# Decode attention for 16 heads on one core: finer last V, first K in three pieces, and V14 rows dealt unevenly

## The chip, the cores and the metric

The kernel runs on one core of a Trainium2 chip. The metric is the device time of one execution in microseconds, the median of several runs; lower is better. Beside it stands one execution recorded by the hardware profiler, whose rows are the profile. The engines are TensorE (PE, its weight loads apart as PEld), VectorE (DVE), ScalarE (ACT), GpSimd (POOL) and SyncE (SP, which issues most transfers); 16 DMA engines move the data.

## The reference

One query row per head attends to 8192 keys. q is (1, 16, 1, 256), k and v are (1, 16, 8192, 256), all bf16.

```python
scale = q.shape[-1] ** -0.5
scores = jnp.einsum("bhqd,bhkd->bhqk", q, k) * scale
p = _softmax(scores, axis=-1)
return jnp.einsum("bhqk,bhkd->bhqd", p, v)
```

## The kernel before

A head's K is 4 MB and so is its V. Both are read from DRAM as 128 partitions of 64 keys ("columns" j = 0 to 63) of 256 values each, so one column is 128 x 512 bytes and a whole head is 32 KB in each partition. Two buffers hold K and two hold V (L86, L87), used by even and odd heads in turn.

**Scores.** VectorE takes columns 0 to 47: for each one a fused multiply with the broadcast q and a sum over the 256 values (L189), which gives one score per partition. TensorE takes columns 48 to 63 in four groups of four: it transposes them (L279), ScalarE copies the transposes from PSUM (L368), TensorE multiplies them with q (L293), and ScalarE copies the 16 scores to S (L372, semaphore "sc"). VectorE then takes the maximum over all 64 columns (L206), TensorE turns it into a row (L227), VectorE reduces it (L173), TensorE broadcasts it (L233), ScalarE forms the exponentials (L380).

**Output.** For each head TensorE runs 64 matmuls, one per column of V, into one PSUM accumulator (`pv`, L258); ScalarE scales the result by the reciprocal of the sum (L393) and sends 512 bytes out (L400).

**Order of the transfers.** One list, `stream` (L57 to L69), written by hand, is issued by SP in its order (L128 to L138). Most entries are a whole head. The first K is cut at column 16 (K_FIRST, L14), V0, V1 and V13 are halved, V14 is cut in four pieces of 16 columns and V15 in seven of 16, 16, 12, 8, 6, 4 and 2 columns (V_LATE, L16). Each late piece has a semaphore of its own (V_SEMS, L18). SP waits before an entry that reuses a buffer: for K, that VectorE is done with the head two before ("kd", L132) and that TensorE has transposed it ("tp", L133); for V, that the matmuls of the head two before are done ("pv", L135). All transfers have 128 rows, one per partition.

**Waits that the change touches.** `head` (L180 to L206) is VectorE's work on one K; it waits for the first piece, at column 16 of head 0 for the rest (L186 to L188), and ahead of the maximum for its own last product (L204) and for "sc" (L205). `pv` (L251) takes a table of waits by column, filled at L348 and L354; at column 32 of V13 and V1 there is one for the second half (L355). GpSimd counts the late semaphores up by 16 at the start (L166), so that the first turns of the loop do not stop at waits meant for the last one.

**q at the start.** ScalarE loads q (L402), TensorE transposes it (L316) and broadcasts each head's row over 128 partitions, two heads per PSUM bank (L328). ScalarE copies them to q_all (L405, L413) and, after the first pair, head 0's 258 columns to q_now (L363), where VectorE and TensorE read them.

Of the kernel before, what the change touches and what calls it, by code (L numbers as in the profile page):

```python
# [6 lines left out]
ACT = mybir.ActivationFunctionType  # L7
# [3 lines left out]

NPE = 16
GRP = 4
K_FIRST = 16  # L14
V_HALVED = 13
V_LATE = {14: (0, 16, 32, 48), 15: (0, 16, 32, 44, 52, 58, 62)}  # L16
AHEAD = {"kd": 1, "sc": 1, "sp": 2, "ex": 2, "m": 1, "g": 1, "mT": 1, "l": 2, "bc": 1, "nb": 1, "rc": 2, "pv": 2, "fin": 4}
V_SEMS = (("va0", "v0b", "v0c", "v0d"), ("va1", "v1b", "v1c", "v1d", "v1e", "v1f", "v1g"))  # L18


class _Step:
# [19 lines left out]
def bass_standalone__mha_softmax__decode_kernel(nc: bass.Bass, q: bass.AP, k: bass.AP, v: bass.AP, out: bass.AP):  # L41
    B, H, Sq, D = q.shape
    Sk = k.shape[2]
    P = 128
    J = Sk // P
# [3 lines left out]
    NG = NPE // GRP  # L49
    JD = J - NPE  # L50
    QW = D + NH
    HALF = J // 2
# [1 line left out]

    stream = [("k", 0, 0, K_FIRST, "k0"), ("k", 0, K_FIRST, J, "k0b"), ("k", 1, 0, J, "k1")]  # L57
    stream += [("v", 0, 0, HALF, "va0"), ("k", 2, 0, J, "k0"), ("v", 0, HALF, J, "v0c")]
    stream += [("v", 1, 0, HALF, "va1"), ("k", 3, 0, J, "k1"), ("v", 1, HALF, J, "v1c")]
    for h in range(2, H):  # L60
# [10 lines left out]
    with contextlib.ExitStack() as ctx:  # L71
# [9 lines left out]
        def sem(name):  # L81
            if name not in sems:
                sems[name] = ctx.enter_context(nc.semaphore(name))
            return sems[name]
# [3 lines left out]
        q_sb = sb("q_sb", [H, D], dt)  # L88
        q_all = sb("q_all", [P, (H + 1) * QW], dt)
        q_now = [sb(f"q_now{i}", [P, QW], dt) for i in range(2)]  # L90
# [3 lines left out]
        m = sb("m", [P, 2], FP32)  # L94
# [14 lines left out]
        sm = ps("sm", [P, 512])  # L109
        qps = ps("qps", [P, 512])  # L110

        for name in ("pool", "cb", "cf", "qp", "qs", "qb", "kd", "tp", "kt", "sp", "sc", "m", "mT", "g", "bc", "nb", "ex"):
            sem(name)
        for name in ("l", "rc", "pv", "fin", "ldq", "k0", "k0b", "k1", "va0", "va1", "v1h", "o0", "o1"):
            sem(name)
        late = [name for row in V_SEMS for name in row[1:] if name not in ("v0c", "v1c")] + ["v1h"]
        for row in V_SEMS:
# [3 lines left out]
        def src(t, h):  # L121
            return t[0, h].rearrange("(p j) d -> p (j d)", p=P)

        if True:

            @(lambda f: f(nc.sync))
            def _(sp):
                for kind, h, a, b, name in stream:  # L128
                    buf = (kbuf if kind == "k" else vbuf)[h % 2]
                    if h >= 2 and a == 0:  # L130
                        if kind == "k":
                            sp.wait_ge(sem("kd"), h)  # L132
                            sp.wait_ge(sem("tp"), (h - 1) * NG)  # L133
                        else:
                            sp.wait_ge(sem("pv"), h + 1)  # L135
                    sp.dma_start(  # L136
                        buf[:, a * D : b * D], src(k if kind == "k" else v, h)[:, a * D : b * D]
                    ).then_inc(sem(name), 16)  # L138
                sp.nop()

            @(lambda f: f(nc.gpsimd))
# [27 lines left out]
            @(lambda f: f(nc.vector))  # L169
            def _(dve):  # L170
                def xmax(h):
                    dve.wait_ge(sem("mT"), h.of(1, 2))
                    dve.tensor_reduce(g[0:1, h.par : h.par + 1], mx[0:1, 0:P], AX.X, ALU.max).then_inc(sem("g"), 1)  # L173

                def recips(h):
                    dve.wait_ge(sem("l"), h.of(1, 3))
                    dve.wait_ge(sem("fin"), h.of(1, 3))
                    dve.reciprocal(recip[0:1, h.par : h.par + 1], qps[0:1, 0:1]).then_inc(sem("rc"), 1)  # L178

                def head(h, at):  # L180
                    dve.wait_ge(sem("qb"), h.of(1, 1))
                    dve.wait_ge(sem("ex"), h.of(1, 1))
                    dve.wait_ge(sem(f"k{h.par}"), h.of(8, 16 - 8 * h.par))
                    buf = kbuf[h.par]
                    for j in range(JD):
                        if j == K_FIRST and h.par == 0:  # L186

                            dve.wait_ge(sem("k0b"), 16)  # L188
                        ins = dve.tensor_tensor_reduce(  # L189
                            out=buf[:, j * D : (j + 1) * D],  # L190
                            in0=buf[:, j * D : (j + 1) * D],
                            in1=q_now[h.par][:, 0:D],
                            scale=SCALE,
                            scalar=0.0,
                            op0=ALU.mult,
                            op1=ALU.add,
                            accum_out=S[h.par][:, j : j + 1],
                        )
                        if j in at:
                            at[j]()  # L200
                    ins.then_inc(sem("kd"), 1)
                    if JD in at:
                        at[JD]()
                    dve.wait_ge(sem("kd"), h.of(1, 2))  # L204
                    dve.wait_ge(sem("sc"), h.of(1, 2))  # L205
                    dve.tensor_reduce(m[:, h.par : h.par + 1], S[h.par][:, :], AX.X, ALU.max).then_inc(sem("m"), 1)  # L206

                with dve.Fori(0, H // 2) as i:  # L208
                    ev, od = _Step(0, i), _Step(1, i)
                    prev = od.back(2)  # L210

                    def later(f, h):
                        with dve.If(i > 0):
                            f(h)

                    head(ev, {2: lambda: later(recips, ev.back(2)), 40: lambda: later(xmax, prev)})
                    head(od, {2: lambda: later(recips, prev), 3: lambda: xmax(ev)})
                last = _Step(H - 1)
                recips(last.back(1))
                xmax(last)  # L220
                recips(last)

            @(lambda f: f(nc.tensor))
            def _(pe):
# [87 lines left out]

                pe.wait_ge(sem("ldq"), 16)
                pe.wait_ge(sem("cb"), 1)
                for hf in range(NH):
                    ins = pe.matmul(  # L316
                        qps[:, hf * H : (hf + 1) * H],
                        lhsT=q_sb[:, hf * P : (hf + 1) * P],
                        rhs=identb[0:H, 0:H],
                        start=True,  # L320
                        stop=True,
                    )
# [15 lines left out]
                with pe.Fori(0, H // 2 + 1) as i:  # L338
                    ev, od = _Step(0, i), _Step(1, i)
                    fin_turn = pe.snap((i // 8) * 16 + 16)  # L340
                    half_turn = pe.snap(((i + 1) // 8) * 16 + 16)
                    old = od.back(2)
                    with pe.If(i < H // 2):
                        scores(ev)
                    with pe.If(i > 0):
                        pv(
                            ev.back(2),
                            {V_LATE[14][n]: [(V_SEMS[0][n], fin_turn)] for n in range(1, len(V_SEMS[0]))},  # L348
                            {32: lambda: transpose_m(old), 48: lambda: bcast(old), 64: lambda: total(old)},
                        )  # L350
                    with pe.If(i < H // 2):
                        scores(od, before=ev)
                    with pe.If(i > 0):
                        waits = {V_LATE[15][n]: [(V_SEMS[1][n], fin_turn)] for n in range(1, len(V_SEMS[1]))}  # L354
                        waits[HALF].append(("v1h", half_turn))  # L355
                        pv(old, waits, {})
                    with pe.If(i < H // 2):
                        total(ev)

            @(lambda f: f(nc.scalar))  # L360
            def _(act):
                def q_copy(h, src_q):
                    act.activation(out=q_now[h.par][:, :], in_=src_q, func=ACT.Copy).then_inc(sem("qb"), 1)  # L363
# [25 lines left out]
                def final(h, dst):  # L389
# [10 lines left out]
                    act.dma_start(dst, o_sb[h.par][0:1, :]).then_inc(sem(f"o{h.par}"), 16)  # L400

                act.dma_start(q_sb[:, :], q[0, :, 0, :]).then_inc(sem("ldq"), 16)  # L402
                by_head = q_all[:, 0 : H * QW].rearrange("p (h w) -> p h w", w=QW)
                act.wait_ge(sem("qp"), 1)
                act.activation(  # L405
                    out=by_head[:, :, D:QW],
                    in_=qps[:, 0 : NH * H].rearrange("p (f h) -> p h f", f=NH),
                    func=ACT.Copy,
                    scale=SCALE,
                )  # L410
                for pair in range(H // 2):
                    act.wait_ge(sem("qp"), pair + 2)
                    ins = act.activation(  # L413
                        out=by_head[:, 2 * pair : 2 * pair + 2, 0:D],
                        in_=acc[pair % 2][:, :].rearrange("p (h d) -> p h d", h=2),
                        func=ACT.Copy,
                    ).then_inc(sem("qs"), 1)
                    if pair == 0:
                        act.wait_ge(sem("qs"), 1)
                        q_copy(_Step(0), q_all[:, 0:QW])  # L420
                act.wait_ge(sem("cf"), 4)
                flat = out.rearrange("b h s d -> (b s) (h d)")
                with act.Fori(0, H // 2) as i:
# [55 lines left out]
```

## Time and profile before

| what | value |
|---|---|
| three runs | 320.09, 320.12, 320.47 us (median 320.12) |
| the profiled execution's own time | 320.24 us |
| its span, first to last instruction | 318.8 us |
| mean granted TensorE clock | 0.85 |
| busy: PE / DVE / ACT / POOL | 215.7 / 275.1 / 92.5 / 1.6 us |
| read from DRAM | 134.23 MB, 421 GB/s over the span |

How to read the profile: times in it are microseconds from the start of the span. A row of a timeline or chain gives start, length, engine, source line, operation and the tiles written and read; behind it in brackets stands the idle time before it and what ended that. SPq rows are issues of transfers; a row "DMA issues" gives how many, KB each, and the time from issue to landing. Windows give the busy time of each engine in a stretch, then the granted PE clock, the mean busy share of the 16 DMA engines, and GB/s; a packet counts with all the time it is open, so a share can pass 1.

### The profile page before, as it was taken

Reading aid. Unit: us, or ns where it says so; the run is one execution under the profiler, and the core shown is the slowest. Engines: PE = TensorE matmul, PEld = TensorE weight load, DVE = VectorE, ACT = ScalarE, POOL = GpSimd, SP = SyncE. Lnnn points to the kernel's source line nnn. Section 1 sums busy time; section 2 is a strip of 40 time slices with the busy share of each in tenths; the row PEclk is TensorE's granted clock in tenths of the full one; section 3 lists DMA queues with packets and bytes.
Section 4 is the critical chain, followed back from the end, with each engine's and each line's share of the span. In section 5 each row is a group of like instructions: output and inputs, shape, how many; then the busy total and the mean of one; then the engine's idle time right before and its main releaser. Section 6 shows DMA issues by size and latency. Waiting matters only on the chain.

```text
span 318.8 us, 6855 instructions
## 1 busy us (share of the span) xinstructions
PE 215.7 (68%) x2162; PEld 154.4 (48%) x2162; DVE 275.1 (86%) x1584; ACT 92.5 (29%) x171; POOL 1.6 (0%) x11
## 2 busy tenths in 40 slices
PE   4427186885685947839388472975839567397996
PEld 1326164664353635626256352653627346265774
DVE  2899999999999998897979979889798897979920
ACT  5436050336015060420504214060230604106010
POOL 1000000000000000000000000000000000000000
PEclk9999999798598786968769598785968969588999
DMA  8999999999999999999999999999999999999994
GB/s 327 455 398 448 399 456 415 419 415 452 428 432 440 419 444 419 444 428 432 436 423 440 415 448 428 432 436 428 440 415 448 419 440 424 436 417 420 417 422 194
DMA packets 6549, 134.29 MB, mean 421 GB/s; under 512 B 752, under 2 KB 912, under 8 KB 1424
## 3 DMA queue, kind: packets, MB, share of 16 engines
q1 hardware_dynamic: 6480, 134.22, 98.5%
q8 instruction: 2, 0.03, 0.0%
q10 hardware_dynamic: 64, 0.02, 0.0%
q14 instruction: 3, 0.02, 0.0%
HBM read 134.23 MB, written 0.01 MB: 421 GB/s over the span
## 4 chain that ended last, share of the span: by engine, by line
DMA 52%; DVE 23%; PE 22%; issue 1%; ACT 1%; SPq 0%; DVEq 0%; ACTq 0%
DMA vbuf<-in_v_dram 48%; DVE kbuf L189 22%; PE acc L258 20%; DMA kbuf<-in_k_dram 4%; DVE S L189 1%; PE sm L233 1%; ACT KT L368 1%; PE mx L227 0%; PE tp L279 0%; SPq L136 0%; PE spe L293 0%; DVE g L173 0%; ACT o_sb L393 0%; DVE recip L178 0%; DVEq L208 0%
## 5 line engine op out<-in xcount | busy, mean ns | idle before, releaser
L189 DVE CUSTOM_DVE_ANT_0 kbuf<-kbuf,q_now 128x256 bf16<-128x256 bf16 x768 | 268.5, 409 | 22.4 <-DMA kbuf<-in_k_dram 21.4
L258 PE MATMUL acc<-vbuf,E 128*1 128x256 bf16 x1024 | 144.6, 310 | 45.2 <-DMA vbuf<-in_v_dram 45.1
L258 PEld LDWEIGHTS acc<-vbuf,E 128*1 128x1 bf16 x1024 | 94.8, 94 | 88.1 <-DMA vbuf<-in_v_dram 46.4
L368 ACT ACTIVATE KT<-tp 128x1024 bf16<-128x1024 bf16 x64 | 62.3, 1021 | 45.9 <-PE tp L279 45.4
L189 DVE DVE_READ_ACCUMULATOR2_ANT S<- 128x1 f32 x768 | 55.0, 72 | 0.0
L279 PE MATMUL tp<-identb,kbuf 128*128 128x128 bf16 x512 | 41.6, 236 | 13.6 <-DMA kbuf<-in_k_dram 13.4
L293 PE MATMUL spe<-q_now,KT 128*128 128x1 bf16 x512 | 22.9, 166 | 27.0 <-ACT KT L368 26.7
L279 PEld LDWEIGHTS tp<-identb,kbuf 128*128 128x128 bf16 x512 | 32.9, 106 | 17.0 <-DMA kbuf<-in_k_dram 11.2
L293 PEld LDWEIGHTS spe<-q_now,KT 128*128 128x128 bf16 x512 | 18.2, 99 | 35.4 <-ACT KT L368 26.4
L393 ACT ACTIVATE o_sb<-acc,recip 1x256 bf16<-1x256 f32 x16 | 7.3, 457 | 83.8 <-PE acc L258 82.6
L376 ACT ACTIVATE negb<-sm 128x1 f32<-128x1 f32 x16 | 2.8, 174 | 87.4 <-PE sm L233 87.4
L173 DVE TENSOR_REDUCE g<-mx 1x1 f32<-1x128 f32 x16 | 4.4, 276 | 7.0 <-PE mx L227 7.0
L227 PE MATMUL mx<-ident,m 128*1 128x128 f32 x32 | 6.3, 279 | 5.8 <-DVE m L206 5.8
L233 PE MATMUL sm<-g,ones_row 1*128 1x1 f32 x32 | 6.4, 268 | 4.7 <-DVE g L173 4.7
L233 PEld LDWEIGHTS sm<-g,ones_row 1*128 1x128 f32 x32 | 5.1, 198 | 6.8 <-DVE g L173 5.3
L363 ACT ACTIVATE q_now<-q_all 128x258 bf16 (+1 forms) x17 | 7.1, 418 | 0.2
L178 DVE RECIPROCAL recip<-qps 1x1 f32<-1x1 f32 x16 | 2.4, 152 | 3.9 <-PE qps L243 3.9
L380 ACT ACTIVATE E<-S,negb 128x64 bf16<-128x64 f32 x16 | 5.6, 348 | 0.5
L227 PEld LDWEIGHTS mx<-ident,m 128*1 128x1 f32 x32 | 2.2, 83 | 6.4 <-DVE m L206 6.0
L328 PE MATMUL acc<-q_sb,identb 16*128 16x256 bf16 x16 | 4.4, 403 | 1.0 <-ACT q_all L413 1.0
L413 ACT ACTIVATE q_all<-acc 128x512 bf16<-128x512 f32 x8 | 4.4, 593 | 0.9 <-PE acc L328 0.9
L372 ACT ACTIVATE S<-spe 128x16 f32<-128x16 f32 x16 | 2.9, 183 | 3.7 <-PE spe L293 3.7
(20 smaller groups left out, 17.1 us busy)
## 6 DMA issues: line engine op xcount, KB each, us to landing
kbuf<-in_k_dram SPq DMA_DIRECT2D x15, 4096.0 KB, 20.5
vbuf<-in_v_dram SPq DMA_DIRECT2D x11, 4096.0 KB, 29.1
vbuf<-in_v_dram SPq DMA_DIRECT2D x6, 2048.0 KB, 24.3
vbuf<-in_v_dram SPq DMA_DIRECT2D x6, 1024.0 KB, 12.9
kbuf<-in_k_dram SPq DMA_DIRECT2D x1, 3072.0 KB, 11.7
kbuf<-in_k_dram SPq DMA_DIRECT2D x1, 1024.0 KB, 4.8
vbuf<-in_v_dram SPq DMA_DIRECT2D x1, 768.0 KB, 11.3
vbuf<-in_v_dram SPq DMA_DIRECT2D x1, 512.0 KB, 12.1
```

The costliest lines, as they stand in the source:

```text
L173: dve.tensor_reduce(g[0:1, h.par : h.par + 1], mx[0:1, 0:P], AX.X, ALU.max).then_inc(sem("g"), 1)
L189: ins = dve.tensor_tensor_reduce(out=buf[:, j * D : (j + 1) * D], in0=buf[:, j * D : (j + 1) * D], in1=q_now[h.par][:, 0:D], scale=SCALE, ...
L227: pe.matmul(mx[0:1, 0:P], lhsT=m[:, h.par : h.par + 1], rhs=ident[:, :], start=True, stop=True).then_inc(sem("mT"), 1)
L233: pe.matmul(sm[:, 0:1], lhsT=ones_row[0:1, 0:P], rhs=g[0:1, h.par : h.par + 1], start=True, stop=True,).then_inc(sem("bc"), 1)
L258: ins = pe.matmul(acc[h.par][0:1, 0:D], lhsT=E[h.par][:, j : j + 1], rhs=vbuf[h.par][:, j * D : (j + 1) * D], start=(j == 0), stop=(j == J ...
L279: ins = pe.transpose(tp[gi % 2][:, b * D + hf * P : b * D + (hf + 1) * P], buf[:, j * D + hf * P : j * D + (hf + 1) * P], identb[:, :],)
L293: ins = pe.matmul(spe[:, c : c + 1], lhsT=KT[gi % 2][:, b * D + hf * P : b * D + (hf + 1) * P], rhs=q_now[h.par][:, D + hf : D + hf + 1], ...
L328: ins = pe.matmul(acc[pair % 2][:, (h % 2) * D : (h % 2 + 1) * D], lhsT=identb[0:H, h : h + 1].to_broadcast([H, P]), rhs=q_sb[:, :], start ...
L363: act.activation(out=q_now[h.par][:, :], in_=src_q, func=ACT.Copy).then_inc(sem("qb"), 1)
L368: act.activation(out=KT[gi % 2][:, :], in_=tp[gi % 2][:, :], func=ACT.Copy).then_inc(sem("kt"), 1)
L380: act.activation(out=E[h.par][:, :], in_=S[h.par][:, :], func=ACT.Exp, bias=negb[:, h.par : h.par + 1], scale=1.0, accum_out=lsum[:, h.par ...
L393: act.activation(out=o_sb[h.par][0:1, :], in_=acc[h.par][0:1, 0:D], func=ACT.Copy, scale=recip[0:1, h.par : h.par + 1],).then_inc(sem("fin ...
```

## The change

- V15 comes in nine pieces of 16, 12, 10, 8, 6, 5, 3, 2 and 2 columns, each with its own semaphore and wait.
- The first K comes in three pieces of 16, 16 and 32 columns; VectorE waits at columns 16 and 32.
- SP's wait for "tp" goes. VectorE waits for "sc" ahead of its last product instead of ahead of the maximum, so "kd" stands for both.
- The second, third and fourth V14 transfers are each issued as three: 112 rows, then the last 16 rows as 9 and 7, 10 and 6, 12 and 4. All three count on the same semaphore, and the wait's value follows (48 more).
- The wait for V1's second half stands at column 28 instead of 32; that for V13's half stays at 32.
- q: a first matmul broadcasts head 0's row into PSUM, ScalarE copies it to q_now at once; head 0's two transposed columns follow from q_all. The activation table is loaded by an instruction of its own.

```diff
-K_FIRST = 16
+K_FIRST = (16, 32)
-V_LATE = {14: (0, 16, 32, 48), 15: (0, 16, 32, 44, 52, 58, 62)}
+V_LATE = {14: (0, 16, 32, 48), 15: (0, 16, 28, 38, 46, 52, 57, 60, 62)}
+V_PARTED = {16: (9, 7), 32: (10, 6), 48: (12, 4)}
...
-    stream = [("k", 0, 0, K_FIRST, "k0"), ("k", 0, K_FIRST, J, "k0b"), ("k", 1, 0, J, "k1")]
+    stream = [("k", 0, 0, K_FIRST[0], "k0"), ("k", 0, K_FIRST[0], K_FIRST[1], "k0a")]
+    stream += [("k", 0, K_FIRST[1], J, "k0b"), ("k", 1, 0, J, "k1")]
...
                             sp.wait_ge(sem("kd"), h)
-                            sp.wait_ge(sem("tp"), (h - 1) * NG)
...
-                    sp.dma_start(
-                        buf[:, a * D : b * D], src(k if kind == "k" else v, h)[:, a * D : b * D]
-                    ).then_inc(sem(name), 16)
+                    rows = V_PARTED.get(a, ()) if (kind, h) == ("v", H - 2) else ()
+                    r = 0
+                    for n in (P - sum(rows),) + rows:
+                        sp.dma_start(
+                            buf[r : r + n, a * D : b * D],
+                            src(k if kind == "k" else v, h)[r : r + n, a * D : b * D],
+                        ).then_inc(sem(name), 16)
+                        r += n
...
-                        if j == K_FIRST and h.par == 0:
-                            dve.wait_ge(sem("k0b"), 16)
+                        if j in K_FIRST and h.par == 0:
+                            dve.wait_ge(sem("k0a" if j == K_FIRST[0] else "k0b"), 16)
+                        if j == JD - 1:
+                            dve.wait_ge(sem("sc"), h.of(1, 2))
...
-                    dve.wait_ge(sem("sc"), h.of(1, 2))
...
+                pe.matmul(
+                    spe[:, 0:D],
+                    lhsT=identb[0:H, 0:1].to_broadcast([H, P]),
+                    rhs=q_sb[:, :],
+                    start=True,
+                    stop=True,
+                ).then_inc(sem("qp"), 1)
...
-                            {V_LATE[14][n]: [(V_SEMS[0][n], fin_turn)] for n in range(1, len(V_SEMS[0]))},
+                            {V_LATE[14][n]: [(V_SEMS[0][n], parted_turn)] for n in range(1, len(V_SEMS[0]))},
...
-                        waits[HALF].append(("v1h", half_turn))
+                        waits[HALF] = [("v1h", half_turn)]
...
+                act.preload_act_table(ACT.Exp)
                 act.wait_ge(sem("qp"), 1)
+                act.activation(out=q_now[0][:, 0:D], in_=spe[:, 0:D], func=ACT.Copy).then_inc(sem("qb"), 1)
+                act.wait_ge(sem("qp"), 2)
...
+                act.wait_ge(sem("qc"), 1)
+                act.activation(out=q_now[0][:, D:QW], in_=q_all[:, D:QW], func=ACT.Copy)
```

More of the change, by code (lines that the diff above doesn't have):

```diff
@@ L13 @@
 GRP = 4
-K_FIRST = 16
+K_FIRST = (16, 32)
 V_HALVED = 13
-V_LATE = {14: (0, 16, 32, 48), 15: (0, 16, 32, 44, 52, 58, 62)}
+V_LATE = {14: (0, 16, 32, 48), 15: (0, 16, 28, 38, 46, 52, 57, 60, 62)}
 AHEAD = {"kd": 1, "sc": 1, "sp": 2, "ex": 2, "m": 1, "g": 1, "mT": 1, "l": 2, "bc": 1, "nb": 1, "rc": 2, "pv": 2, "fin": 4}
-V_SEMS = (("va0", "v0b", "v0c", "v0d"), ("va1", "v1b", "v1c", "v1d", "v1e", "v1f", "v1g"))
+V_PARTED = {16: (9, 7), 32: (10, 6), 48: (12, 4)}
+V_SEMS = (("va0", "v0b", "v0c", "v0d"), ("va1", "v1b", "v1c", "v1d", "v1e", "v1f", "v1g", "v1i", "v1j"))
 class _Step:
@@ L110, in bass_standalone__mha_softmax__decode_kernel @@
         qps = ps("qps", [P, 512])
-        for name in ("pool", "cb", "cf", "qp", "qs", "qb", "kd", "tp", "kt", "sp", "sc", "m", "mT", "g", "bc", "nb", "ex"):
+        for name in ("qc", "pool", "cb", "cf", "qp", "qs", "qb", "kd", "tp", "kt", "sp", "sc", "m", "mT", "g", "bc", "nb", "ex"):
             sem(name)
-        for name in ("l", "rc", "pv", "fin", "ldq", "k0", "k0b", "k1", "va0", "va1", "v1h", "o0", "o1"):
+        for name in ("l", "rc", "pv", "fin", "ldq", "k0", "k0a", "k0b", "k1", "va0", "va1", "v1h", "o0", "o1"):
             sem(name)
@@ L340, in _ @@
                     fin_turn = pe.snap((i // 8) * 16 + 16)
+                    parted_turn = pe.snap((i // 8) * 48 + 16)
                     half_turn = pe.snap(((i + 1) // 8) * 16 + 16)
@@ L409, in _ @@
                     scale=SCALE,
-                )
+                ).then_inc(sem("qc"), 1)
+                act.wait_ge(sem("qc"), 1)
+                act.activation(out=q_now[0][:, D:QW], in_=q_all[:, D:QW], func=ACT.Copy)
                 for pair in range(H // 2):
-                    act.wait_ge(sem("qp"), pair + 2)
-                    ins = act.activation(
+                    act.wait_ge(sem("qp"), pair + 3)
+                    act.activation(
                         out=by_head[:, 2 * pair : 2 * pair + 2, 0:D],
@@ L417, in _ @@
                     ).then_inc(sem("qs"), 1)
-                    if pair == 0:
-                        act.wait_ge(sem("qs"), 1)
-                        q_copy(_Step(0), q_all[:, 0:QW])
                 act.wait_ge(sem("cf"), 4)
```

## The prediction

> **What bounds the kernel now.** I read the page first, then stretches of the span by window, then the chain that ended last, then single issues.
>
> ```profile
> span 318.8 us, 6855 instructions
> DMA  8999999999999999999999999999999999999994
> q1 hardware_dynamic: 6480, 134.22, 98.5%
> ```
>
> The transfers run from the first slice to the last: K and V, 134.22 MB, pass through one queue whose packets take 98.5% of all 16 DMA engines' time. A change inside the stream counts only if it starves the queue, makes bytes dearer or alters the two ends. The next view gives stretches of the span (length, PE busy, PE clock, DMA share, GB/s).
>
> ```profile
> 140.00:280.00 140.00, 93.87 (x949) 66.98 (x950) 124.48 (x718) 37.14 (x67) 0.00 (x0) 0.78 1.00 432
> 300.00:314.00 14.00, 13.14 (x120) 9.53 (x119) 4.56 (x26) 1.54 (x5) 0.00 (x0) 1.00 1.01 415
> ...
> 313.00:314.00 1.00, 0.88 (x9) 0.46 (x8) 0.00 (x0) 0.00 (x0) 0.00 (x0) 1.00 1.00 378
> 314.00:314.50 0.50, 0.50 (x7) 0.40 (x5) 0.00 (x0) 0.00 (x0) 0.00 (x0) 1.00 0.61 229
> 314.50:315.00 0.50, 0.50 (x7) 0.37 (x6) 0.00 (x0) 0.00 (x0) 0.00 (x0) 1.00 0.42 162
> 315.00:315.50 0.50, 0.50 (x7) 0.39 (x5) 0.00 (x0) 0.00 (x0) 0.00 (x0) 1.00 0.38 141
> 315.50:316.00 0.50, 0.50 (x7) 0.39 (x5) 0.00 (x0) 0.00 (x0) 0.00 (x0) 1.00 0.14 47
> ```
>
> The steady rate is 432 GB/s, 27 GB/s for each of 16 engines, so 4 MB take 9.71 us, and a V14 row of 8 KB takes one engine 0.303 us. The end is ragged. After 314.0 the shares fall from 1.00 to 0.61, 0.42, 0.38 and 0.14: about eight engines are done by 314.3, two more by 315, and six (0.38 of 16) run into the last half microsecond. What is left at 314.0 is 0.5 x (0.61 + 0.42 + 0.38 + 0.14) = 0.78 us of all 16; shared evenly it would end at 314.8 instead of near 315.9. Now the chain at the end (start, length, what), the last two output rows, and two of V15's issues with their times to landing.
>
> ```profile
> 301.48 9.88 DMA vbuf<-in_v_dram
> 311.37 0.04 issue
> 311.41 1.91 PE acc L258 x16
> 313.32 0.12 issue
> 313.44 3.67 PE acc L258 x32
> 317.11 0.03 ACTq L392
> ...
> 317.18 0.46 ACT o_sb L393
> ```
>
> ```profile
> 301.96 0.43 SPq L136 DMA_DIRECT2D vbuf<-in_v_dram  x1
> ...
> vbuf<-in_v_dram SPq DMA_DIRECT2D x1, 768.0 KB, 11.3
> ...
> 303.86 0.43 SPq L136 DMA_DIRECT2D vbuf<-in_v_dram  x1
> ...
> vbuf<-in_v_dram SPq DMA_DIRECT2D x1, 128.0 KB, 12.6
> ```
>
> V15's third piece lands at 301.96 + 11.3 = 313.26, its last at 303.86 + 12.6 = 316.46 (call this T): 20 columns in 3.2 us, 0.16 us a column, while TensorE takes 3.67 / 32 = 0.115. TensorE therefore waits for 16 columns at 311.37 and 12 at 313.26, and then works off 32 columns without a pause until 317.11, 0.65 us after T. Behind that lie 318.8 - 317.1 = 1.7 us (the scaling, the output's transfer) that the diff does not touch, and 320.24 - 318.8 = 1.4 us outside the span. So the time is T, plus TensorE's lag behind T, plus constants.
>
> **The change part by part.**
>
> *V15 in nine pieces.* The boundaries become 16, 28, 38, 46, 52, 57, 60, 62. At 0.16 us a column the pieces that end at columns 28, 38, 46, 52, 57, 60, 62, 64 land at T minus 5.8, 4.2, 2.9, 1.9, 1.1, 0.6, 0.3, 0. Following TensorE at 0.115 us a column with 0.1 us for each wait that a landing ends (0.04 and 0.12 in the chain), it finishes column 28 at T - 4.3, 38 at T - 2.9, 46 at T - 1.9, 52 at T - 1.1, 57 at T - 0.4, 60 at T - 0.1, 62 at T + 0.1 and 64 at T + 0.4. Its lag falls from 0.65 to 0.4: **-0.25 us**. The ends: 0 if the waits eat it, -0.4 if they cost nothing. Two more waits stand on PE and only its own columns are behind them; two more issues of SP (0.47 us each, from the spacing of the rows above) come by 304.9, ten us ahead of their landing, and nothing is behind them. Pool's two extra counts at the start have until the last V.
>
> *Three V14 transfers in 112 rows plus two parts.* A 128-row transfer leaves 6480 / 45 = 144 packets: 128 rows, eight per engine, and 16 small ones. 112 rows are seven per engine. Nothing in the trace shows who takes a part of 9 or 7 rows; I choose one row each on the first 9, the first 7, and so on, and that the eight early engines are the first. Then engines 0 to 3 carry three rows more than before, 4 and 5 two, 6 one, 7 and 8 none; 9 carries one fewer, 10 and 11 two fewer, 12 to 15 three fewer. In time, 3 x 0.303 = 0.91 and 2 x 0.303 = 0.61. The early engines move from 314.1 - 314.3 to at most 315.0 - 315.2; the late six from 315.5 - 316.0 to 314.6 - 315.4. The last packet ends near 315.2 instead of 315.9, so T falls by **0.75 us**. The ends: -1.1 with the even finish at 314.8, and +5.5 (second rival).
>
> [...]
>
> More transfers cost more: in 300 to 314, with pieces of 1 MB and less, the rate is 415 against 432, 4% of 14 us or 0.55 us over some ten transfers, 0.05 each. I count four such (two pieces, six small parts taken as two): **+0.2 us** (0 to 0.4). SP issues V14 as ten transfers from 287.1 on, ending near 291.8; V15's issue waits until 301.1 for another reason (the chain row at 301.48 starts behind it), so nothing is late.
>
> *First K in 16, 16, 32.*
>
> ```profile
> 5.12 0.42 ACT L363 ACTIVATE q_now<-q_all 128x258 bf16<-128x258 bf16 x1
> ...
> 5.71 0.43 DVE L189 CUSTOM_DVE_ANT_0 kbuf<-kbuf,q_now 128x256 bf16<-128x256 bf16 x1 [5.71 <-DMA kbuf<-in_k_dram]
> ...
> 12.89 0.42 DVE L189 CUSTOM_DVE_ANT_0 kbuf<-kbuf,q_now 128x256 bf16<-128x256 bf16 x1 [1.56 <-DMA kbuf<-in_k_dram]
> ...
> 24.07 0.33 SPq L136 DMA_DIRECT2D kbuf<-in_k_dram  x1
> 24.08 0.22 DVE L206 TENSOR_REDUCE m<-S 128x1 f32<-128x64 f32 x1
> ```
>
> VectorE stands still for 1.56 us for the 48-column piece. A 1 MB piece landing about 2.4 us after the first removes that, so K0 ends near 22.4, and K2, issued when K0 is done (24.07), goes out 1.6 us earlier. K1 lands at about 23.1 (next fence), so VectorE then gains only 1.0 us on K1 and K2, and K4 (58.82) goes out about 1.0 us earlier. Does an earlier issue matter? Compare landings (KB, us from issue to landing):
>
> ```profile
> kbuf<-in_k_dram SPq DMA_DIRECT2D x1, 4096.0 KB, 21.5
> vbuf<-in_v_dram SPq DMA_DIRECT2D x1, 2048.0 KB, 26.6
> 1.63 0.42 SPq L136 DMA_DIRECT2D kbuf<-in_k_dram  x1
> 2.10 0.56 SPq L136 DMA_DIRECT2D vbuf<-in_v_dram  x1
> ```
>
> ```profile
> kbuf<-in_k_dram SPq DMA_DIRECT2D x1, 4096.0 KB, 14.7
> 24.07 0.33 SPq L136 DMA_DIRECT2D kbuf<-in_k_dram  x1
> ```
>
> ```profile
> vbuf<-in_v_dram SPq DMA_DIRECT2D x1, 2048.0 KB, 21.6
> 41.13 0.33 SPq L136 DMA_DIRECT2D kbuf<-in_k_dram  x1
> 41.50 0.43 SPq L136 DMA_DIRECT2D vbuf<-in_v_dram  x1
> ```
>
> ```profile
> kbuf<-in_k_dram SPq DMA_DIRECT2D x1, 4096.0 KB, 14.1
> 58.82 0.33 SPq L136 DMA_DIRECT2D kbuf<-in_k_dram  x1
> ```
>
> V0's first half lands at 2.10 + 26.6 = 28.7 and K2, next in the queue, at 38.8: 10.07 us for 4 MB instead of 9.71. V1's second half lands at 63.1 and K4 at 72.9: 9.8. So the queue loses about 0.4 us at K2 and 0.1 us at K4, both issued late. I take **-0.2 us** back; the ends are 0 (the loss has another cause) and -0.5.
>
> *The rest, at nothing.* The new first matmul and the 256-column copy give VectorE its q earlier than 5.54 (5.12 + 0.42), but VectorE's first row above says that the transfer of K0 released it, so at most the 0.17 us between 5.54 and 5.71 is in it, and K1's landing takes that back. An explicit load of the activation table takes the place of one that the first copy caused. SP's wait for PE's transposes goes and VectorE waits for the score copy one step earlier, ahead of the last product instead of ahead of the maximum:
>
> ```profile
> L206 DVE TENSOR_REDUCE m<-S 128x1 f32<-128x64 f32 x16 | 3.5, 220 | 0.5
> ```
>
> 0.5 us of idle over 16 maxima: the copy is always there first. Were it late, one product (0.35 us) would follow the wait, and SP's next K behind it. V1's second half is now waited for at column 28 instead of 32; it landed at 63.1 and that product starts at 65.78:
>
> ```profile
> 65.78 4.42 PE L258 MATMUL acc<-vbuf,E 128*1 128x256 bf16 x39
> ```
>
> **The sum**, on the profiled execution: 320.24 - 0.25 - 0.75 + 0.2 - 0.2 = 319.24. The three runs have a median of 320.12, 0.12 below that execution, so about 319.1. I leave the first K's part at its middle and say **319.1 us**, with a range of its own from 318.7 to 319.5.
>
> **The rivals.**
>
> *The full gain.* The rows even out the engines (T 1.1 us earlier), the first K's part brings its 0.5 and the lag 0.4: 320.12 - 1.1 - 0.5 - 0.4 + 0.1 = 318.2, and with half of each excess 318.6. For it: the sum of the shares. Against it: engines 0 to 3 go too far by my own rows. Chance 0.08.
>
> *The rows do not meet the late engines.* If the late six are not those that lose rows, T stays and only the finer pieces and K count: 320.12 - 0.25 - 0.2 + 0.2 = 319.9, between 319.5 and 320.3. For it: no row names an engine. Against: the split of eight early and eight late looks like two halves. Chance 0.17.
>
> *The parts queue on the partitions they write: slower.* All parts write into the last 16 partitions, and 112 rows deal seven to an engine where it was eight. [...] For it: every transfer in the trace but the smallest has 128 rows and the even rate may hang on that. Against: the bytes per partition stay the same. Chance 0.20.
>
> [...]
>
> **How the numbers follow.** Forecast 0.55, full gain 0.08, no meeting 0.17, slower 0.20. The measurement tells 0.2% or 0.64 us from no change, so faster is below 319.48 and slower above 320.76. Faster is the forecast but its upper edge and the full gain: 0.61. Same is the rest and nearly all of the second rival: 0.20. Slower: 0.19. The range reaches from 318.4 to 321.6: below it lies half of the full gain, above it most of the slower rival, together some 0.17.
>
> **What would show it.** The q1 queue holds 45 transfers of 128 rows again (45 x 144 packets), three of 112 (3 x 128) and 48 parted rows: 6480 + 384 + 48 + 48 = 6960 packets if each part uses as many engines as it has rows, 7008 if all 16 answer for each. The shares after the first drop at the end should fall from 1 to 0 within 1.3 us, not 2. VectorE's 1.56 us at 12.9 should be gone and K2 out at 22.4, K4 near 57.8. TensorE should end 0.4 us after the last landing. Wrong would be: V14's pieces landing later than 2.5 us apart (third rival), or the same six engines late (second).

## The result and the profile after

The changed kernel takes 329.58 us (median of 6 runs, 328.75 to 330.17), the kernel before 320.32 us on the same chip; the ratio is 1.0288, with a 95% interval of 1.0277 to 1.0299. It is slower by 9.3 us: the direction of the third rival, which had a chance of 0.20. The profiled execution took 329.36 us with a span of 327.9.

From the page of the changed kernel:

```profile
span 327.9 us, 6839 instructions
...
DMA  8999999999999999999999999999999999999993
GB/s 321 445 416 436 420 446 410 434 440 444 432 412 440 444 432 412 440 444 432 416 436 444 432 416 436 444 436 412 436 444 436 416 432 444 408 424 266 232 350 132
...
q1 hardware_dynamic: 6960, 134.22, 98.2%
```

The DMA engines look as busy as before in every slice, but the rate row shows where the time went: 36 slices as before, then 266, 232 and 350 GB/s. The packets are 6960, the number worked out for parts that each run on as many engines as they have rows. Stretches of the changed kernel (length, PE, PEld, DVE, ACT, POOL busy, PE clock, DMA share, GB/s):

```profile
140.00:280.00 140.00, 94.17 (x949) 67.31 (x950) 124.45 (x717) 37.14 (x67) 0.00 (x0) 0.78 1.00 431
...
290.00:300.00 10.00, 8.16 (x87) 5.96 (x84) 10.00 (x59) 2.86 (x8) 0.00 (x0) 1.00 1.01 358
300.00:310.00 10.00, 4.16 (x37) 2.71 (x35) 4.35 (x25) 0.46 (x1) 0.00 (x0) 1.00 1.02 233
...
310.00:320.00 10.00, 7.56 (x52) 4.90 (x52) 0.16 (x1) 1.08 (x4) 0.00 (x0) 0.83 1.00 331
320.00:322.00 2.00, 1.90 (x17) 1.18 (x16) 0.00 (x0) 0.00 (x0) 0.00 (x0) 1.00 0.92 344
322.00:323.00 1.00, 0.99 (x10) 0.57 (x8) 0.00 (x0) 0.00 (x0) 0.00 (x0) 1.00 0.53 193
323.00:324.00 1.00, 1.00 (x10) 0.63 (x11) 0.00 (x0) 0.00 (x0) 0.00 (x0) 1.00 0.13 50
324.00:325.00 1.00, 1.00 (x9) 0.57 (x8) 0.00 (x0) 0.00 (x0) 0.00 (x0) 1.00 0.06 23
325.00:326.00 1.00, 1.00 (x11) 0.50 (x8) 0.00 (x0) 0.00 (x0) 0.00 (x0) 1.00 0.02 8
```

From 140 to 280 the rate is what it was (431 against 432). While the parted transfers run, from 300 to 310, it is 233 with a DMA share of 1.02; the kernel before has 421 with a share of 1.01 in the same stretch, so the share alone does not show the rate:

```profile
300.00:310.00 10.00, 9.85 (x92) 7.42 (x91) 4.56 (x26) 1.54 (x5) 0.00 (x0) 1.00 1.01 421
```

The end is also more ragged, not less: the shares take more than 3 us to go from 0.9 to nothing, and the 0.06 after 324 is one engine of 16 that runs on alone. The chain that ended last, in the changed kernel:

```profile
301.00 20.63 DMA vbuf<-in_v_dram
321.63 0.04 issue
321.68 1.25 PE acc L265 x10
322.93 0.01 issue
322.94 3.29 PE acc L265 x26
326.23 0.03 ACTq L407
```

And its issues of V14's first transfer, which the diff does not alter, and of V15's last, each with the time to landing; the rows of the same V14 transfer follow from the run named whole V14 below, which is the changed kernel without the parts.

```profile
286.37 0.33 SPq L140 DMA_DIRECT2D vbuf<-in_v_dram  x1
...
vbuf<-in_v_dram SPq DMA_DIRECT2D x1, 1024.0 KB, 14.5
...
306.87 1.17 SPq L140 DMA_DIRECT2D vbuf<-in_v_dram  x1
...
vbuf<-in_v_dram SPq DMA_DIRECT2D x1, 128.0 KB, 18.9
```

```profile
286.18 0.33 SPq L140 DMA_DIRECT2D vbuf<-in_v_dram  x1
...
vbuf<-in_v_dram SPq DMA_DIRECT2D x1, 1024.0 KB, 12.7
```

The last landing T is 306.87 + 18.9 = 325.8, against 316.5: all of the 9.3 us. TensorE ends at 326.23, 0.46 after T, as the prediction's term for the nine pieces had it (0.4). And V14's first transfer, whole and with its full 128 rows, lands at 286.37 + 14.5 = 300.9, against 286.18 + 12.7 = 298.9 without the parts: 2.0 us later, though only what stands behind it in the queue differs. The trace's landing records of single engines give the rest: V14's four pieces are complete at 300.9, 305.8, 310.9 and 315.9, about 5 us apart, against 298.9, 301.4, 303.9 and 306.4 with V14 whole. Pieces more than 2.5 us apart were the prediction's own sign for its third rival.

### The profile page after: what moved, and what is told of

It is laid out like the page before. It is cut to its first block, busy times and chain, and to the rows that moved or that the text cites. A ratio compares the mean times of both kernels' runs of the same rounds, so it can differ in the third digit from the quotient of the medians.

```text
span 327.9 us, 6839 instructions
## 1 busy us (share of the span) xinstructions
PE 218.6 (67%) x2163; PEld 155.2 (47%) x2163; DVE 275.2 (84%) x1584; ACT 92.5 (28%) x172; POOL 1.6 (0%) x11
## 3 DMA queue, kind: packets, MB, share of 16 engines
q1 hardware_dynamic: 6960, 134.22, 98.2%
## 4 chain that ended last, share of the span: by engine, by line
DMA 66%; PE 18%; DVE 14%; SPq 1%; issue 1%; ACT 0%; DVEq 0%; ACTq 0%
DMA vbuf<-in_v_dram 59%; PE acc L265 18%; DVE kbuf L197 13%; DMA kbuf<-in_k_dram 6%; SPq L140 1%; DVE S L197 0%; DVE g L179 0%; PE sm L240 0%; ACT o_sb L408 0%; DVE recip L184 0%; DVEq L215 0%; DVEq L189 0%; PE qps L250 0%; DVE m L213 0%; ACTq L407 0%
## 5 line engine op out<-in xcount | busy, mean ns | idle before, releaser
L286 PE MATMUL tp<-identb,kbuf 128*128 128x128 bf16 x512 | 42.3, 239 | 15.7 <-DMA kbuf<-in_k_dram 15.4
L286 PEld LDWEIGHTS tp<-identb,kbuf 128*128 128x128 bf16 x512 | 33.7, 107 | 19.2 <-DMA kbuf<-in_k_dram 13.5
L378 ACT ACTIVATE q_now<-q_all 128x258 bf16 x16 | 6.7, 419 | 0.1
L213 DVE TENSOR_REDUCE m<-S 128x1 f32<-128x64 f32 x16 | 3.5, 220 | 0.5
```

The source lines that it names most:

```text
L286: ins = pe.transpose(tp[gi % 2][:, b * D + hf * P : b * D + (hf + 1) * P], buf[:, j * D + hf * P : j * D + (hf + 1) * P], identb[:, :],)
```

## The experiments

The theory to be tried, a supposition of mine: the parts and the 112-row pieces reach too few partitions at once, so engines wait for each other where they write. Its rivals: the finer V15 or the first K is to blame; parts are dear because they are small and run on few engines; the late engines got rows. The diffs show the main lines only; the value of the wait, the extra buffer and its semaphore follow from them.

**Whole V14.** The changed kernel with the parts taken out.

```diff
-V_PARTED = {16: (9, 7), 32: (10, 6), 48: (12, 4)}
+V_PARTED = {}
```

> The changed kernel with the three V14 transfers whole again (128 rows); all else as changed. Theory (the parted transfers queue on the partitions that they write): the whole loss goes with them and the other terms of the prediction remain, so 319.4 to 319.9 us. Rival (finer V15 pieces or the first K do it): it stays above 325 us.

Measured: 320.15 us (11 runs), ratio to before 0.9995, interval 0.9986 to 1.0004. The whole loss goes with the parts; of the small gains expected of the rest, 0.15 us is seen, within the uncertainty. Its last issue and the end of its chain:

```profile
303.84 0.43 SPq L140 DMA_DIRECT2D vbuf<-in_v_dram  x1
...
vbuf<-in_v_dram SPq DMA_DIRECT2D x1, 128.0 KB, 12.7
```

```profile
312.38 1.25 PE acc L265 x10
313.63 0.02 issue
313.65 3.31 PE acc L265 x26
316.96 0.03 ACTq L407
```

T is 303.84 + 12.7 = 316.5, where it was, and TensorE ends 0.4 us after it instead of 0.65. So the shorter lag is there, and T gives nothing.

**Parts only.** The kernel before with V_PARTED, its loop over row ranges and the wait's value, nothing else.

```diff
+V_PARTED = {16: (9, 7), 32: (10, 6), 48: (12, 4)}
...
+                    rows = V_PARTED.get(a, ()) if (kind, h) == ("v", H - 2) else ()
...
+                    for n in (P - sum(rows),) + rows:
...
+                    parted_turn = pe.snap((i // 8) * 48 + 16)
```

> The kernel before with the three V14 transfers parted as in the change and nothing else. Theory: 329.5 to 330.5 us, the loss and a little more. Rival (the loss needs the finer V15 behind it, whose issues took SP longer): below 324 us.

Measured: 329.72 us (328.83 to 330.64), ratio 1.029 (1.0268 to 1.0311). The parts alone are the loss; the finer V15 has no share in it.

**One parted transfer.**

```diff
-V_PARTED = {16: (9, 7), 32: (10, 6), 48: (12, 4)}
+V_PARTED = {48: (12, 4)}
```

> The changed kernel with only the fourth V14 transfer parted (112, 12 and 4 rows), the second and third whole. Theory: each parted transfer is dear by itself, a third of the loss of about 9.4 us, so 323.0 to 323.6 us. Rival (the loss builds up only when one parted transfer meets the next): under 321.5 us.

Measured: 323.76 and 325.22 us, 3.6 and 5.1 us above whole V14, both more than the third of the loss (3.1 us) that I expected. A parted transfer is dear by itself; two runs 1.5 us apart do not say by how much more than a third.

**112 and 16 rows.** By the row counts every engine has 7 + 1 rows, so the load is even and no part runs on few engines.

```diff
-V_PARTED = {16: (9, 7), 32: (10, 6), 48: (12, 4)}
+V_PARTED = {16: (16,), 32: (16,), 48: (16,)}
```

> The changed kernel with the three V14 transfers as 112 and 16 rows, which is one more row for every engine, so that all 16 carry 8 rows as before. [...] Rival (the uneven load on the low engines and the parts' few engines do it): 319.4 to 320 us.

Measured: 328.32 us, ratio 1.0242 (1.0226 to 1.0258). The uneven load and the few engines are not the cause: with an even load on all engines 8.2 of the 9.4 us remain. No record shows which partitions of the 112 rows an engine gets.

**64 and 64 rows, two ways.** Lower and upper half of the partitions, then even and odd partitions. By the row counts both give every engine 4 + 4 rows.

```diff
-V_PARTED = {16: (9, 7), 32: (10, 6), 48: (12, 4)}
+V_PARTED = {16: (64,), 32: (64,), 48: (64,)}
```

> The changed kernel with the three V14 transfers as 64 and 64 rows: four rows to each of 16 engines each time, no small part, even load. [...] Rival (small parts and uneven loads): 319.4 to 320 us.

```diff
+V_PARTED = {16: 2, 32: 2, 48: 2}
...
+                    step = V_PARTED.get(a, 1) if (kind, h) == ("v", H - 2) else 1
+                    for r in range(step):
+                        sp.dma_start(
+                            buf[r : r + P - step + 1 : step, a * D : b * D],
+                            src(k if kind == "k" else v, h)[r : r + P - step + 1 : step, a * D : b * D],
+                        ).then_inc(sem(name), 16)
```

> The changed kernel with the three V14 transfers each as the 64 even and the 64 odd partitions, four rows to an engine, instead of the lower and the upper 64. If what counts is how much of the 128 partitions one transfer reaches, 320.2 to 321 us. If what counts is which engines write neighbouring partitions at the same time, and a transfer of 64 rows no longer gives each engine partitions of its own, a loss like that of 64 and 64, above 326 us.

Measured: halves 329.58 us, ratio 1.0287 (1.0271 to 1.0302); even and odd 320.22 us, ratio 1.0001 (0.9989 to 1.0012). The same bytes, rows, engines and number of transfers differ by 9.4 us. The stretch from 300 to 310, halves first, then even and odd:

```profile
300.00:310.00 10.00, 5.17 (x47) 3.48 (x44) 4.55 (x27) 0.47 (x1) 0.00 (x0) 1.00 1.00 225
```

```profile
300.00:310.00 10.00, 10.00 (x95) 7.61 (x94) 4.65 (x28) 1.40 (x5) 0.00 (x0) 1.00 1.01 417
```

225 GB/s is about half of the steady 432. At half of the steady rate three transfers of 1 MB would cost 7.3 us more (an estimate, 3 x 2.43 us at 432 GB/s), and 9.4 were measured. In the landing records V14's unchanged first transfer is complete at 301.95 instead of 298.91, so the loss begins ahead of the three transfers that I counted. My second reading for even and odd fell: the loss like that of the halves does not come. Between these two runs the reach decides: half of the partitions in one block, or every second one of all. How the rows are dealt to the engines is not in the trace, and the runs with eight rows below show that reach is not all that counts.

**Extra rows to an unread buffer.** The next four leave V14 whole and add transfers behind each of its last three, so that rows, sizes and engines can be held fixed while the partitions change; they read 384 KB more. First the change's own parts, to the last 16 partitions and then to every fourth partition:

```diff
+V_EXTRA = {16: (9, 7), 32: (10, 6), 48: (12, 4)}
...
+                            sp.dma_start(
+                                xb[r : r + n, x : x + 16 * D], src(v, h)[r : r + n, a * D : b * D]
+                            ).then_inc(sem("xs"), 16)
```

> The changed kernel with V14 whole, and behind each of the three transfers two extra ones into a buffer that nobody reads: 9 and 7, 10 and 6, 12 and 4 rows of 8 KB, written to partitions 112 to 127. It adds 384 KB to what is read. Theory (engines that write neighbouring partitions wait for each other): well above the next run, 2.5 us or more, 324 us or over. Rival (a part is dear because it is small or runs on few engines): as the next run.

```diff
-                                xb[r : r + n, x : x + 16 * D], src(v, h)[r : r + n, a * D : b * D]
+                                xb[at : at + 4 * n - 3 : 4, x : x + 16 * D], src(v, h)[r : r + n, a * D : b * D]
```

> The same extra transfers with the same row counts, sizes and source rows, written to every fourth partition from 0 and from 64, so that no two rows of a part lie in one group of four. Theory: engines 0 to 3 carry six rows more, 6 x 0.303 = 1.8 us, so about 322 us, and no more. Rival: as the run before, whatever it gives.

Measured: 326.86 and 323.74 us. Both runs read the same rows from DRAM in the same sizes, so the 3.1 us between them come from the partitions that are written; the second is still 1.7 us above what six rows more on engines 0 to 3 explain (an estimate, 6 x 0.303 us above whole V14). Then one row for each of the 16 engines, again to the last 16 partitions first:

```diff
+V_EXTRA = {16: (16,), 32: (16,), 48: (16,)}
...
+                                xb[r : r + n, x : x + 16 * D], src(v, h)[r : r + n, a * D : b * D]
```

> The changed kernel with V14 whole and, behind each of its last three transfers, one extra transfer of 16 rows, one row for each engine, into an unread buffer in partitions 112 to 127. The load is even: 3 x 0.303 = 0.9 us. [...] Rival: 321.2 us.

```diff
-                                xb[r : r + n, x : x + 16 * D], src(v, h)[r : r + n, a * D : b * D]
+                                xb[at : at + 8 * n - 7 : 8, x : x + 16 * D], src(v, h)[r : r + n, a * D : b * D]
```

> As the run with 16 extra rows, written to every eighth partition instead. [...] Rival: the same as that run.

Measured: 325.38 and 322.87 us: 5.2 and 2.7 us above whole V14, 0.9 of it load by my estimate (3 x 0.303 us). The last 16 partitions are the dearest again; every eighth partition is not free either, with 1.8 us above the load. Why is not shown.

**Eight rows on the first eight engines, two places.** Two extra transfers of 8 rows behind each of three V14 transfers, to every fourth partition from 0 and 32, then from 64 and 96. The trace does not number the engines: "the first eight" are those that take a part of eight rows.

```diff
+V_EXTRA = {16: (8, 8), 32: (8, 8), 48: (8, 8)}
...
+                        for at, n in zip((0, 0 + 32), V_EXTRA[a]):
...
+                                xb[at : at + 29 : 4, x : x + 16 * D], src(v, h)[r : r + n, a * D : b * D]
```

> The changed kernel with V14 whole and, behind each of its last three transfers, two extra ones of 8 rows into an unread buffer, to every fourth partition from 0 and from 32. If a part runs on the first engines, engines 0 to 7 carry six rows more, 6 x 0.303 = 1.8 us. If the late engines are among the others, that fits into the 1.8 us by which the early ones are ahead: 320.2 to 321.0 us. If late engines are among the first eight: 321.8 us or more.

```diff
-                        for at, n in zip((0, 0 + 32), V_EXTRA[a]):
+                        for at, n in zip((64, 64 + 32), V_EXTRA[a]):
```

> The same rows on the same engines, written to every fourth partition from 64 and from 96 instead. [...] Rival (only the engines' own load counts): the same as the run before.

Measured, on the same chip: 321.94 us, ratio 1.0047 (1.0032 to 1.0062), and 325.61 us, ratio 1.0158 (1.0139 to 1.0176). Transfers of the same rows and row counts are 3.7 us apart. Stretches from 296 to 314, first from 0 and 32, then from 64 and 96:

```profile
296.00:314.00 18.00, 16.79 (x151) 12.37 (x149) 8.55 (x50) 1.54 (x5) 0.00 (x0) 0.99 1.01 416
```

```profile
296.00:314.00 18.00, 13.35 (x104) 9.07 (x104) 8.52 (x50) 1.54 (x5) 0.00 (x0) 0.91 1.01 341
```

```profile
296.00:314.00 18.00, 17.14 (x157) 12.62 (x155) 8.56 (x50) 1.54 (x5) 0.00 (x0) 1.00 1.01 417
```

In the first place the rate is that of whole transfers (417 for the kernel before from 296 to 314, in the last fence): an extra row then costs its engine some 0.3 us (below) and nobody else. In the second the whole queue slows to 341 GB/s, although each part takes every fourth partition as in the first. So it also matters which partitions a part of eight rows writes; why is not shown. The parts of 9 and 7 rows and their like on every fourth partition were written from 64 too (378 GB/s from 296 to 314), which may be the 1.7 us left over there. The first run also answers where the late engines are. Its chain ends so:

```profile
314.27 4.55 PE acc L274 x36
318.82 0.03 ACTq L416
```

TensorE ends at 318.82, against 316.96 with V14 whole: 1.86 us, six rows of 0.31. So the engine that ends last carries the extra rows: it is one of the first eight. The trace's landing records of single engines in this run say the same; the first line is V14's second transfer on 16 engines (first to last landing, us), the others its two extra ones on eight engines each:

```text
299.32 299.44 299.48 299.54 299.58 299.60 299.61 299.69 299.71 299.74 299.75 299.93 300.55 301.04 301.11 301.41
299.90 299.91 299.92 300.02 300.05 300.23 300.86 301.73
300.20 300.22 300.24 300.34 300.37 300.54 301.16 302.04
```

The records do not say which of the two extra transfers a landing is of; I split them so that each of the second follows one of the first by 0.30 to 0.32. Four engines are late in the first line, by about 0.9 to 1.8 us. Two of them, those at 300.55 and at 301.41, come back 0.31 and 0.32 later in the second line, so they are among the first eight; the other two are not.

**Rows moved with reach.** One, then two of V14's transfers in six parts each. Every part takes every second or every fourth partition; if the parts of eight run on the first eight engines, these get 10 rows and the others 6.

```diff
+V_STRIDED = (48,)
...
+                        parts = [slice(1, P, 2), slice(2, P, 4)] + [slice(n, n + 29, 4) for n in (0, 32, 64, 96)]
```

> The changed kernel with V14's second and third transfers whole and the fourth as six: 64 odd partitions, 32 of every fourth from 2, and four times 8 of every fourth from 0, 32, 64 and 96. If parts of 8 run on the first eight engines, these carry 10 rows and the others 6. Each part reaches at least eight separate groups of four partitions. If the late engines are among the others and the reach is what counts: 0.6 us less in T, 0.2 more for five more transfers, so 319.7 to 319.9 us against 320.15 with V14 whole. If the parts still hold each other up: 320.5 us or more.

```diff
-V_STRIDED = (48,)
+V_STRIDED = (32, 48)
```

> The same with the third and fourth transfers: four rows moved, 1.2 us. By the same sum the last engines come 1.2 us earlier and the first eight 1.2 us later, so T falls by about 0.8 net of the transfers: 319.4 to 319.7 us. If the parts hold each other up: above the run with one.

Measured: 321.94 us, ratio 1.0039 (1.0026 to 1.0053), and 324.10 us, ratio 1.011 (1.0095 to 1.0126). A loss that grows with the number moved. Two causes fit: the engine that ends last gets rows, 0.6 us for each transfer, and parts of 8 rows from 64 and 96 slow the queue, as the run before showed (341 GB/s). The first alone is too small: against whole V14 by their ratios the runs lose some 1.4 and 3.7 us, and the rate from 296 to 314 falls to 396 and 369 GB/s from 413. How much is due to each the runs do not say.

**The other two terms alone**, on the kernel before: V15 in nine pieces, and the first K in three.

```diff
-V_LATE = {14: (0, 16, 32, 48), 15: (0, 16, 32, 44, 52, 58, 62)}
+V_LATE = {14: (0, 16, 32, 48), 15: (0, 16, 28, 38, 46, 52, 57, 60, 62)}
```

> The kernel before with V15 in the nine pieces and nothing else. My term: TensorE's lag behind the last landing falls by 0.25 us and two more transfers cost 0.1, so 0.15 us less than before, ratio 0.9995. Rival (more transfers cost as much as the lag gives): 1.000.

```diff
-K_FIRST = 16
+K_FIRST = (16, 32)
```

> The kernel before with the first K in 16, 16 and 32 columns and nothing else. My term: K2 out at 22.4, K4 at 57.9, and 0.2 us less, ratio 0.9994. Rival (the last engines are late for another reason than late issues): K2 and K4 go out earlier, the last landing stays at 316.4 and the ratio at 1.000.

Measured: ratio 0.9996 (0.9987 to 1.0005) and 1.0001 (0.9993 to 1.001). Neither can be told from no change. In the run with the first K alone, K2 and K4 do go out earlier, and the shares at the end change in an instructive way:

```profile
22.41 0.33 SPq L137 DMA_DIRECT2D kbuf<-in_k_dram  x1
...
58.04 0.33 SPq L137 DMA_DIRECT2D kbuf<-in_k_dram  x1
```

```profile
314.00:314.50 0.50, 0.50 (x7) 0.38 (x5) 0.00 (x0) 0.00 (x0) 0.00 (x0) 1.00 0.51 186
314.50:315.00 0.50, 0.50 (x8) 0.37 (x6) 0.00 (x0) 0.00 (x0) 0.00 (x0) 1.00 0.26 96
315.00:315.50 0.50, 0.50 (x7) 0.40 (x5) 0.00 (x0) 0.00 (x0) 0.00 (x0) 1.00 0.20 74
315.50:316.00 0.50, 0.50 (x7) 0.37 (x6) 0.00 (x0) 0.00 (x0) 0.00 (x0) 1.00 0.09 29
```

Between 314.5 and 315.5 the share is 0.26 and 0.20 instead of 0.42 and 0.38: about four engines are late where there were six. But the last of them ends where it did, and the last one sets the time.

No version here beats the kernel before by more than the measurement is uncertain.

## Why the prediction was wrong

- **The parted transfers (-0.75 us) are the step that failed.** I took them as rows moved between engines at 0.303 us each and kept the rate of the queue. Every run with V14 cut into blocks of neighbouring partitions loses rate (225 to 258 GB/s from 300 to 310, or 235 from 296 to 314 for the parts only); even and odd (417) and whole V14 (413 from 296 to 314) do not. In place of -0.75 us the parts cost +9.4 us (329.58 against 320.15).
- **The third rival had the direction right.** That the partitions written decide, the runs show: the same extra rows took 326.86 us in the last 16 partitions and 323.74 on every fourth. How engines share partitions they do not show, and no run shows the +5.5 us at the upper end of the parts' term, which is this rival's; the runs showed +9.4 us for all three parted transfers and 3.6 and 5.1 us for one. Without a price of their own were the 112-row pieces and the transfer ahead: 112 and 16 rows, which have an even load, already cost 8.2 us, and V14's unchanged first transfer lands 2.0 us later. No run has the 112-row pieces alone. Sixteen extra rows in the last 16 partitions cost 5.2 us, 0.9 of it their load; if the two add, an estimate of 3.9 us is left for the 112 rows. I also counted as evidence against it that the bytes per partition stay the same. They do, and it did not help: halves and even and odd rows have the same bytes per partition too.
- **The assumption that the early eight are the first eight was wrong too.** The engine that ends last is one of the eight that take a part of eight rows, so even without the loss it would not have been relieved. The choice that parts run on the same few engines each time held as far as the runs show it (6960 packets, both eight-row parts on one group of engines, 0.31 us apart). The second rival's condition was thus true as well, hidden below the third. By my own dealing the eight get up to three rows more, so T would have stayed or risen by as much as 0.9 us.
- **V15 in nine pieces (-0.25 us)** was right: the lag is 0.4 to 0.46 instead of 0.65. With V15 alone the last landing comes at 316.52 instead of 316.42 in the landing records, the 0.1 us that I took for two more transfers. Some 0.15 us of the sum is left, in whole V14 and in V15 alone, both within the uncertainty.
- **The first K (-0.2 us)** failed as a time though its steps came as worked out: K2 at 22.2 and K4 at 57.9 in the changed kernel (forecast 22.4 and 57.8). I read the late landings of K2 and K4 as a loss of the whole queue. By the shares at the end, their earlier issue brings some two engines forward, and not the one that ends last; why that one is late stays open.
- The covers of the edits at nothing held: the maxima still idle 0.5 us in all, and whole V14 shows no new wait.

## What to carry to other kernels

Cut a transfer by columns rather than by blocks of partitions: 64 and 64 rows as halves cost 9.4 us over three 1 MB transfers. Even and odd rows cost nothing (320.22 us), but smaller parts in wider steps did lose (1.4 and 3.7 us), so a cut by rows has to be tried. A full DMA share did not mean full rate (1.02 at 233 GB/s): read GB/s beside it. Before evening out engines, find out which are late; a few rows on a known group of engines, written where they do no harm (416 GB/s here), show it in one run.

## What the runs showed of the hardware that was not expected

- From 300 to 310, transfers to half of the partitions in one block moved 225 GB/s, to every second partition 417.
- Parts of eight rows cost the eight engines that take them 0.31 us a row when written to every fourth partition from 0 and 32 (416 GB/s went on), and the whole queue slowed to 341 GB/s when they were written from 64 and 96.
- The loss reaches backward: a whole transfer ahead of the parted ones, issued at nearly the same time, landed at 300.9 instead of 298.9.
- With the parts in the queue SP's last issue took 1.17 us (306.87) instead of 0.43. It still came 18.9 us ahead of its landing, so it cost nothing here.
